# Decode attention over a 512 MB cache: loads of 8 MB for pairs of heads, `wo` loaded once at the end, MLP first

## The chip, the cores and the metric

The kernel runs on one NeuronCore of a Trainium2 chip. The metric is the device time of one execution in microseconds (us), the median of several runs. Before the change it is 1318.7 us (three runs, 1317.83 to 1319.73).

## What is computed

One decode step for two sequences. `x` (2 x 1 x 512) is layer-normalised to `xn`. Attention takes `q = xn @ wq` as 32 heads of 128, scores it against a cache of 8192 keys for each of the 64 (sequence, head) units, applies softmax, takes the weighted sum of 8192 values and multiplies by `wo`. A small MLP on the same `xn` makes a gate:

```
q = (xn @ wq) as [B=2, H=32, 1, Dh=128]
p = softmax(q . k_cache * Dh**-0.5)          # k_cache [2, 32, 8192, 128] float32
s = (p @ v_cache) as [2, 1, 4096] @ wo       # v_cache likewise, wo [4096, 512]
g = silu(gelu(layernorm(xn) @ w1 + b1) @ w2 + b2)
out = x + s * g
```

K and V are 268 MB each. With the weights the kernel reads 559.3 MB from device memory and writes 4 KB.

## The kernel before, in words

Everything is float32. The 64 units are taken in order, the two sequences of a head one after the other. A unit's keys are one tile of [128 partitions x 64 rows x 128], 4 MB: partition p holds rows 64p to 64p+63, so each partition's row in memory is 32 KB in one piece (`unit`, L50). `load_k` (L56) and `load_v` (L71) issue one transfer per unit from the SP queue. There are three K buffers and two V buffers of 32 KB per partition. `wo` comes in eight loads of 1 MB (`load_wo`, L60), one per four heads, in rows of 2 KB; the last head's 256 KB come by themselves at L325. The last unit's V comes in five pieces (L69).

Work of one unit:

- VectorE (DVE) multiplies the K tile in place by the query, which stands on every partition (L250), sums over the 128 elements (L254), and takes the row maximum (L256).
- TensorE (PE) transposes the 128 maxima (L260), DVE reduces them to one (L265), PE spreads it back (L270), and ScalarE (ACT) copies it and takes the exponential with a running sum (L272, L275). PE sums that over the partitions (L277) and DVE takes the reciprocal (L282).
- `weighted` (L285): sixteen matmuls with the probabilities as the stationary operand (128 x 4) and 512 columns of V moving, spread over four column groups of PE. Each appears as two records in the trace, so 32 records a unit.
- `project` (L296): ACT copies the result out of PSUM (L300), four small matmuls fold it to a column (L305), ACT scales it (L308). After the second sequence of a head four matmuls add its share of `wo` to `acc` (L314).

The order is written out by hand (L317 to L348), and each engine and each queue works in program order. In step i the SP queue gets the loads of K i+3 and V i+1; DVE multiplies unit i, PE and ACT do the softmax of unit i-1, DVE sums unit i, and PE weighs V of unit i-2. A load waits until its buffer is free: a K load until DVE has summed the unit that held the buffer, a V load until PE has weighed it. A load that waits holds back all later loads on SP.

Ahead of the loop come `x`, `wq` in two loads of 4 MB, K 0, `w1`, K 1, `w2`, K 2, the first `wo` and V 0; the layer norms; the projection of the queries (L163) and their spreading to all partitions, four heads at a time (L176). The MLP runs in pieces inside steps 0 to 2 (L339 to L343). After the loop the last unit is weighed, projected and added, then L355 and L356 multiply by the gate and add `x`, and four small stores (L359) end the kernel.

Of the kernel before, what the change touches and what calls it, by code (L numbers as in the profile page):

```python
# [19 lines left out]
def decode_kernel(ctx: ExitStack, tc: tile.TileContext, x, kc, vc, wq, wo, w1, b1, w2, b2, out):  # L20
# [18 lines left out]
    consts = ctx.enter_context(tc.tile_pool(name="consts", bufs=1))
    kpool = ctx.enter_context(tc.tile_pool(name="kpool", bufs=3))  # L40
    vpool = ctx.enter_context(tc.tile_pool(name="vpool", bufs=2))
    wpool = ctx.enter_context(tc.tile_pool(name="wpool", bufs=2))
    small = ctx.enter_context(tc.tile_pool(name="small", bufs=3))
    ps_c = ctx.enter_context(tc.tile_pool(name="ps_c", bufs=1, space=bass.MemoryType.PSUM))
    ps_w = ctx.enter_context(tc.tile_pool(name="ps_w", bufs=2, space=bass.MemoryType.PSUM))
    ps_s = ctx.enter_context(tc.tile_pool(name="ps_s", bufs=3, space=bass.MemoryType.PSUM))
# [3 lines left out]
    def unit(t, i):  # L50
        h, b = divmod(i, B)
        return t[b, h].rearrange("(p j) d -> p j d", p=P)

    K, V, WO = {}, {}, {}

    def load_k(i):  # L56
        K[i] = kpool.tile([P, KP, DH], F32, tag="k", name=f"k{i}")
        nc.sync.dma_start(K[i], unit(kc, i))

    def load_wo(g):  # L60
        t = wpool.tile([P, HG, D], F32, tag="w", name=f"wo{g}")
        src = wo[g * HG * DH:(g + 1) * HG * DH, :].rearrange("(h p) n -> p h n", p=P)
        n = HG if g < NG - 1 else HG - 1
        nc.sync.dma_start(t[:, :n, :], src[:, :n, :])
        WO[g] = t
        return t, src


    PIECES = [(0, 16), (16, 16), (32, 16), (48, 12), (60, 4)]  # L69

    def load_v(i):  # L71
        V[i] = vpool.tile([P, KP, DH], F32, tag="v", name=f"v{i}")
        if i < NU - 1:
            nc.sync.dma_start(V[i], unit(vc, i))  # L74
        else:
            for k0, n in PIECES:
                nc.sync.dma_start(V[i][:, k0:k0 + n, :], unit(vc, i)[:, k0:k0 + n, :])

    x_sb = consts.tile([B, D], F32, name="x_sb")
    nc.sync.dma_start(x_sb, x.rearrange("b s d -> (b s) d"))  # L80

    wq_v = wq.rearrange("(p c) n -> p c n", p=P)
    WQ = []
    for a in range(0, ND, 2):
        t = vpool.tile([P, 2, H * DH], F32, tag="v", name=f"wq{a}")
        nc.sync.dma_start(t, wq_v[:, a:a + 2, :])
        WQ.append(t)
    load_k(0)
    w1_sb = kpool.tile([P, ND, F], F32, tag="k", name="w1_sb")
    nc.sync.dma_start(w1_sb, w1.rearrange("(p c) f -> p c f", p=P))  # L90
    load_k(1)
    w2_sb = vpool.tile([P, NF + 1, D], F32, tag="v", name="w2_sb")
    nc.sync.dma_start(w2_sb[:, :NF, :], w2[:NF * P, :].rearrange("(p c) n -> p c n", p=P))
    nc.sync.dma_start(w2_sb[:FT, NF, :], w2[NF * P:, :])
    load_k(2)
    load_wo(0)
    load_v(0)
# [4 lines left out]
    b2_sb = consts.tile([1, D], F32, name="b2_sb")  # L102
    nc.vector.memset(x4, 0.0)
    nc.vector.memset(b1_sb, 0.0)
    for j in range(QT):
        nc.scalar.dma_start(x4[32 * j:32 * j + B, :], x[:, 0, j * P:(j + 1) * P])
# [7 lines left out]
    ones = consts.tile([P, P], F32, name="ones")  # L114
    nc.vector.memset(ones, 1.0)
    zeros = consts.tile([P, P], F32, name="zeros")
    nc.vector.memset(zeros, 0.0)
    srow = consts.tile([1, P], F32, name="srow")
# [4 lines left out]
    mask = consts.tile([P, JW], F32, name="mask")  # L123

    PO = [ps_c.tile([P, JW * DH], F32, name=f"po{n}") for n in range(2)]
    for t in PO:
        nc.vector.memset(t, 0.0)
    acc = ps_c.tile([P, P], F32, name="acc")


    def layernorm(src, name):
# [7 lines left out]
        dst = consts.tile([B, D], F32, name=name)  # L139
        nc.vector.tensor_scalar(dst, src, mv[:, 0:1], sd[:, 1:2], op0=ALU.subtract, op1=ALU.mult)  # L140
        return dst

    def transposed(src, name):
# [3 lines left out]
        for c in range(ND):  # L147
# [4 lines left out]
    xn = layernorm(x_sb, "xn")  # L152
    nc.vector.tensor_reduce(out=mask, in_=ident.rearrange("p (j r) -> p r j", r=32)[:, :JW, :],
                            axis=AX.X, op=ALU.add)
    y = layernorm(xn, "y")
# [3 lines left out]

    q_nat = consts.tile([P, NG // QT, 512], F32, name="q_nat")  # L160
    nc.gpsimd.memset(q_nat, 0.0)

    def project_q(n):  # L163
        p = ps_w.tile([P, 512], F32, tag="w", name=f"pq{n}")
        for c in range(ND):
            for j in range(QT):
                g = n * QT + j
                nc.tensor.matmul(p[32 * j:32 * j + B, :], xnT[:, c, :],  # L168
                                 WQ[c // 2][:, c % 2, g * 512:(g + 1) * 512],
                                 start=(c == 0), stop=(c == ND - 1))  # L170
        for j in range(QT):
            nc.scalar.copy(q_nat[32 * j:32 * j + B, n, :], p[32 * j:32 * j + B, :])  # L172

    Q = {}

    def queries(g):  # L176

        n, j = divmod(g, QT)
        q = small.tile([P, B, HG, DH], F32, tag="q", name=f"q{g}", bufs=2)
        for b in range(B):  # L180
            p = ps_w.tile([P, 512], F32, tag="w", name=f"pb{g}_{b}")
            r = 32 * j + b
            nc.tensor.matmul(p, ident[:, r:r + 1].to_broadcast([P, P]), q_nat[:, n, :], start=True, stop=True)  # L183
            nc.scalar.copy(q[:, b].rearrange("p h d -> p (h d)"), p)
        Q[g] = q

    project_q(0)
    queries(0)
    project_q(1)
    nc.tensor.matmul(acc, zeros, zeros, start=True, stop=False)  # L190


    gate = consts.tile([P, P], F32, name="gate")
    hT = consts.tile([P, NF + 1, B], F32, name="hT")
    G = {}

    def mlp_hidden():

        p = ps_s.tile([P, P], F32, tag="s", name="ph")
        nc.vector.memset(p[:, :(NF + 1) * B], 0.0)  # L200
        for f in range(NF + 1):
            for c in range(ND):
                w = w1_sb[:, c, f:NF * P:NF] if f < NF else w1_sb[:, c, NF * P:]
                nc.tensor.matmul(p[:w.shape[1], f * B:(f + 1) * B], w, yT[:, c, :],  # L204
                                 start=(c == 0), stop=(c == ND - 1))
        G["ph"] = p

    def mlp_gelu():
# [3 lines left out]
        p = G.pop("ph")[:, :(NF + 1) * B].rearrange("p (f b) -> p f b", b=B)  # L212
# [8 lines left out]

    def mlp_out():
        p = ps_s.tile([P, P], F32, tag="s", name="pgate")
        nc.tensor.matmul(p, zeros, zeros, start=True, stop=False)
        for f in range(NF + 1):
            m = P if f < NF else FT
            for j in range(QT):
                nc.tensor.matmul(p[32 * j:32 * j + B, :], hT[:m, f, :], w2_sb[:m, f, j * P:(j + 1) * P],
                                 start=False, stop=False)
        for j in range(QT):  # L230
            nc.tensor.matmul(p[32 * j:32 * j + B, :], ones[:1, :B], b2_sb[:, j * P:(j + 1) * P],
                             start=False, stop=True)
        G["pg"] = p

    def mlp_silu():
        z = small.tile([P, P], F32, tag="gz", name="gz", bufs=1)
        nc.scalar.copy(z, G.pop("pg"))
        th = small.tile([P, P], F32, tag="gt", name="gt", bufs=1)
# [4 lines left out]

    SC, PR, RS, RL, MX, OT = {}, {}, {}, {}, {}, {}

    def scores_mul(i):
        h, b = divmod(i, B)
        k = K[i]
        qb = Q[h // HG][:, b, h % HG, :].unsqueeze(1).to_broadcast([P, KP, DH])
        nc.vector.tensor_tensor(out=k, in0=k, in1=qb, op=ALU.mult)  # L250

    def scores_sum(i):
        SC[i] = small.tile([P, KP], F32, tag="sc", name=f"sc{i}")
        nc.vector.tensor_reduce(out=SC[i], in_=K.pop(i), axis=AX.X, op=ALU.add)  # L254
        MX[i] = small.tile([P, 1], F32, tag="mx", name=f"mx{i}")
        nc.vector.tensor_reduce(out=MX[i], in_=SC[i], axis=AX.X, op=ALU.max)  # L256

    def max_pe(i):
        p = ps_s.tile([P, P], F32, tag="s", name=f"pm{i}")
        nc.tensor.transpose(p[:1, :], MX[i], ident)  # L260
        MX[i] = p

    def max_dve(i):
        nm = small.tile([1, 1], F32, tag="nm", name=f"nm{i}")
        nc.vector.tensor_reduce(out=nm, in_=MX[i][:1, :], axis=AX.X, op=ALU.max, negate=True)  # L265
        MX[i] = nm

    def exps(i):
        p = ps_s.tile([P, P], F32, tag="s", name=f"pn{i}")
        nc.tensor.matmul(p[:, :1], srow, MX.pop(i), start=True, stop=True)  # L270
        bias = small.tile([P, 1], F32, tag="bias", name=f"bias{i}")
        nc.scalar.copy(bias, p[:, :1])  # L272
        PR[i] = small.tile([P, KP], F32, tag="pr", name=f"pr{i}")
        RS[i] = small.tile([P, 1], F32, tag="rs", name=f"rs{i}")
        nc.scalar.activation(PR[i], SC.pop(i), AF.Exp, bias=bias, scale=SCALE, accum_out=RS[i])  # L275
        pl = ps_s.tile([P, P], F32, tag="s", name=f"pl{i}")
        nc.tensor.matmul(pl[:, :1], ones, RS.pop(i), start=True, stop=True)  # L277
        RL[i] = pl
# [38 lines left out]
    for i in range(NU + 1):  # L317
# [8 lines left out]

        if i < NU:
            scores_mul(i)
# [58 lines left out]
```

## Time and profile before

| | |
|---|---|
| median of 3 runs | 1318.7 us |
| the profiled execution | 1319.86 us, of which the span from first to last instruction is 1318.1 us |
| busy share of the span | DVE 87%, PE 44% (weight loads 17%), ACT 8%, GpSimd 0% |
| mean share of the 16 DMA engines | 9 tenths or more in every slice of the span but the last (6 tenths) |
| read from device memory | 559.30 MB, mean 425 GB/s over the whole span |
| packets on SP's queue | 23948 |
| mean granted TensorE clock | 0.643 |

How to read it: the page cuts the span into 40 slices of 33 us. DMA share and GB/s per slice say whether the transfers ever stop. A row of part 5 is a group of instructions of one line: count, busy time, mean duration, then the idle time of the engine just before them and what ended most of it. The chain (part 4) is followed back from the last instruction to whatever released each step.

### The profile page before, as it was taken

How to read it: one execution, taken by the hardware profiler on the slowest of the kernel's cores; microseconds unless marked ns; L12 is line 12 of the kernel's file. 1: busy time of each engine (PE TensorE's matmuls, PEld its weight loads, DVE VectorE, ACT ScalarE, POOL GpSimd, SP SyncE). 2: the span in 40 equal slices, each digit the busy share in tenths (PEclk: the TensorE clock that was granted, in tenths of full speed). 3: DMA queues.
4: the chain of work that ended last, by engine and by line, in shares of the span. 5: the costliest groups of instructions: out<-in, count | busy, mean ns of one | idle time of the engine just before them, and what ended most of it. 6: DMA issues, size and time to landing. Idle time of an engine off the chain costs nothing.

```text
span 1318.1 us, 8108 instructions
## 1 busy us (share of the span) xinstructions
PE 586.5 (44%) x3434; PEld 226.1 (17%) x3434; DVE 1143.7 (87%) x348; ACT 110.7 (8%) x353; POOL 1.6 (0%) x7
## 2 busy tenths in 40 slices
PE   3554444335434344435435435435344345335336
PEld 0431111112111111111111112111111111111112
DVE  1789999888988988988988988988988889998983
ACT  1010010001000010000000001000000001000001
POOL 0000000000000000000000000000000000000000
PEclk9656676666567667576666567666566566666667
DMA  9999999999999999999999999999999999999996
GB/s 392 421 424 431 432 432 427 431 431 433 430 428 429 432 432 433 428 430 431 432 430 427 432 432 429 433 425 436 432 429 428 431 430 432 428 432 431 431 431 252
DMA packets 24266, 559.83 MB, mean 425 GB/s; under 512 B 2611, under 2 KB 2627, under 8 KB 7078
## 3 DMA queue, kind: packets, MB, share of 16 engines
q1 hardware_dynamic: 23948, 559.30, 99.1%
q8 instruction: 27, 0.44, 0.1%
q10 hardware_dynamic: 282, 0.01, 0.0%
q14 instruction: 9, 0.07, 0.0%
HBM read 559.30 MB, written 0.00 MB: 424 GB/s over the span
## 4 chain that ended last, share of the span: by engine, by line
DMA 64%; DVE 27%; PE 8%; ACT 1%; issue 0%; SPq 0%; DVEq 0%
DMA k<-in_A_k_cache_dram 55%; DVE k L250 15%; DVE sc L254 11%; DMA v<-in_A_v_cache_dram 8%; PE po L292 5%; PE ph L204 1%; DMA wq<-in_A_wq_dram 1%; PE pb L183 1%; PE pn L270 0%; PE pl L277 0%; PE pt L305 0%; ACT pr L275 0%; DVE nm L265 0%; SPq L74 0%; ACT o L300 0%
## 5 line engine op out<-in xcount | busy, mean ns | idle before, releaser
L250 DVE TENSOR_TENSOR k<-k,q 128x8192 f32<-128x8192 f32 x64 | 556.2, 8691 | 135.6 <-DMA k<-in_A_k_cache_dram 109.9
L254 DVE TENSOR_REDUCE sc<-k 128x64 f32<-128x8192 f32 x64 | 554.9, 8671 | 0.0
L292 PE MATMUL po<-v,pr 128*4 128x512 f32 x2046 | 353.6, 853 | 10.3 <-DMA v<-in_A_v_cache_dram 10.3
L270 PE MATMUL pn<-nm,srow 1*128 1x1 f32 x128 | 36.8, 354 | 571.7 <-DVE nm L265 571.7
L270 PEld LDWEIGHTS pn<-nm,srow 1*128 1x128 f32 x128 | 31.8, 307 | 585.3 <-DVE nm L265 423.7
L292 PEld LDWEIGHTS po<-v,pr 128*4 128x4 f32 x2046 | 58.0, 107 | 255.2 <-issue 243.5
L305 PE MATMUL pt<-mask,o 128*128 128x1 f32 x512 | 67.4, 253 | 45.7 <-ACT o L300 45.7
L305 PEld LDWEIGHTS pt<-mask,o 128*128 128x128 f32 x512 | 61.9, 191 | 108.1 <-ACT o L300 108.1
L300 ACT COPY o<-po 128x512 f32<-128x512 f32 x64 | 37.5, 586 | 395.4 <-PE po L292 395.4
L272 ACT COPY bias<-pn 128x1 f32<-128x1 f32 x64 | 10.2, 159 | 667.1 <-PE pn L270 667.1
L277 PE MATMUL pl<-rs,ones 128*128 128x1 f32 x128 | 37.5, 362 | 47.4 <-ACT pr L275 47.4
L277 PEld LDWEIGHTS pl<-rs,ones 128*128 128x128 f32 x128 | 32.0, 311 | 52.9 <-ACT pr L275 52.9
L183 PE MATMUL pb<-q_nat,ident 128*128 128x512 f32 x32 | 29.9, 1089 | 2.6 <-ACT q_nat L172 2.6
L265 DVE TENSOR_REDUCE nm<-pm 1x1 f32<-1x128 f32 x64 | 17.4, 272 | 13.4 <-PE pm L260 13.4
L204 PE MATMUL ph<-yT,w_sb 128*128 128x2 f32 (+1 forms) x88 | 19.5, 359 | 13.7 <-DVE ph L200 13.7
L308 ACT ACTIVATE oT<-pt,rl 128x1 f32<-128x1 f32 x64 | 16.7, 262 | 74.0 <-PE pt L305 71.7
L275 ACT ACTIVATE pr<-sc,bias 128x64 f32<-128x64 f32 x64 | 22.3, 348 | 2.1
L204 PEld LDWEIGHTS ph<-yT,w_sb 128*128 128x128 f32 (+1 forms) x88 | 19.4, 316 | 13.8 <-DVE ph L200 13.8
L314 PE MATMUL acc<-wo,oT 128*2 128x128 f32 x256 | 14.7, 307 | 11.2 <-ACT oT L308 11.2
L260 PE MATMUL pm<-ident,mx 128*1 128x128 f32 x64 | 18.6, 290 | 0.7 <-DVE mx L256 0.6
L168 PE MATMUL pq<-wq,xnT 128*2 128x512 f32 x64 | 11.7, 883 | 10.7 <-DMA wq<-in_A_wq_dram 10.7
L256 DVE TENSOR_REDUCE mx<-sc 128x1 f32<-128x64 f32 x64 | 14.1, 220 | 2.2
(65 smaller groups left out, 83.9 us busy)
## 6 DMA issues: line engine op xcount, KB each, us to landing
k<-in_A_k_cache_dram SPq DMA_DIRECT2D x64, 4096.0 KB, 40.8
v<-in_A_v_cache_dram SPq DMA_DIRECT2D x63, 4096.0 KB, 32.3
wq<-in_A_wq_dram SPq DMA_DIRECT2D x2, 4096.0 KB
wo<-in_A_wo_dram SPq DMA_DIRECT2D x7, 1024.0 KB, 43.4
v<-in_A_v_cache_dram SPq DMA_DIRECT2D x3, 1024.0 KB, 9.0
w_sb<-in_B_w_dram SPq DMA_DIRECT2D x1, 2752.0 KB
w_sb<-in_B_w_dram SPq DMA_DIRECT2D x1, 2560.0 KB
wo<-in_A_wo_dram SPq DMA_DIRECT2D x1, 768.0 KB, 42.4
```

Source lines behind the costliest of these rows:

```text
L183: nc.tensor.matmul(p, ident[:, r:r + 1].to_broadcast([P, P]), q_nat[:, n, :], start=True, stop=True)
L204: nc.tensor.matmul(p[:w.shape[1], f * B:(f + 1) * B], w, yT[:, c, :], start=(c == 0), stop=(c == ND - 1))
L250: nc.vector.tensor_tensor(out=k, in0=k, in1=qb, op=ALU.mult)
L254: nc.vector.tensor_reduce(out=SC[i], in_=K.pop(i), axis=AX.X, op=ALU.add)
L260: nc.tensor.transpose(p[:1, :], MX[i], ident)
L265: nc.vector.tensor_reduce(out=nm, in_=MX[i][:1, :], axis=AX.X, op=ALU.max, negate=True)
L270: nc.tensor.matmul(p[:, :1], srow, MX.pop(i), start=True, stop=True)
L275: nc.scalar.activation(PR[i], SC.pop(i), AF.Exp, bias=bias, scale=SCALE, accum_out=RS[i])
L277: nc.tensor.matmul(pl[:, :1], ones, RS.pop(i), start=True, stop=True)
L292: nc.tensor.matmul(po[32 * j:32 * j + JW, :], PR[i][:, t * JW:(t + 1) * JW], v[:, t * JW:(t + 1) * JW, :].rearrange("p j d -> p (j d)"), s ...
L300: nc.scalar.copy(o4, PO[i % 2])
L305: nc.tensor.matmul(pt[:, :1], lhsT, rhs, start=(n == 0), stop=(n == len(terms) - 1))
```

## The change

The unit becomes a pair of neighbouring heads of one sequence (n = 0 to 31, the first sequence's sixteen pairs first). Its K and its V are one load of 8 MB each: 128 partitions with 128 rows of 128, one head on partitions 0 to 63 and the other on 64 to 127, 64 KB in one piece per partition. Two buffers of 64 KB per partition hold K (and at first `wq`, at the end V 30 and `wo`), one holds V (and at first all that the MLP and the projection need, in `boot`).

- DVE's two large operations are done in halves of 64 rows, so each keeps the shape it had (128 x 8192); per pair there are two multiplies and two sums. The first pair's K comes in two halves.
- The softmax steps run once per pair: one transpose, one maximum with two results, two small matmuls, one copy, two exponentials on 64 partitions each, written into a tile `PZ` that is zero elsewhere, so that one matmul with 8 stationary columns weighs both heads. `weighted` is now 32 matmuls per pair.
- The heads' results are not multiplied by `wo` one by one. `columns`, `spread` and `place` put each pair's result into a PSUM tile `OA` that is laid out for one multiplication at the end; the denominators are collected there too. `wo` is one tile of 64 KB rows, in five pieces, the last load of the kernel; 128 matmuls on it follow the last pair.
- The MLP runs whole before the projection, with `w1` and `w2` loaded before `wq`. `load_k(1)` and `load_v(0)` stand behind the projection in SP's queue.
- In the loop, step n issues on SP `load_v(n)` once pair n-1 is weighed, and `load_k(n+2)` at its end; the last steps have an order of their own (`LATE` is 30).

The core of the diff:

```diff
+    U = 2
+    HP = P // U
+    KP = S // HP
+    HH = H // U
+    N = B * HH
...
+    kpool = ctx.enter_context(tc.tile_pool(name="kpool", bufs=2))
+    vpool = ctx.enter_context(tc.tile_pool(name="vpool", bufs=1))
...
+    def load_k(n, cuts=(0, KP)):
+        K[n] = kpool.tile([P, KP, DH], F32, tag="k", name=f"k{n}")
+        load(K[n], kf[n], cuts)
+
+    def load_v(n, cuts=(0, KP), pool=vpool, tag="v"):
+        V[n] = pool.tile([P, KP, DH], F32, tag=tag, name=f"v{n}")
+        load(V[n], vf[n], cuts)
+
+
+    PIECES = (0, 32, 64, 96, 112, 128)
+    WO_PIECES = (0, 8, 16, 24, 29, 32)
...
+    wq_sb = kpool.tile([P, ND, H * DH], F32, tag="k", name="wq_sb")
+    boot = vpool.tile([P, KP * DH], F32, tag="v", name="boot")
...
     nc.sync.dma_start(x_sb, x.rearrange("b s d -> (b s) d"))
 
     nc.sync.dma_start(w1_sb, w1.rearrange("(p c) f -> p c f", p=P))
     nc.sync.dma_start(w2_sb[:, :NF, :], w2[:NF * P, :].rearrange("(p c) n -> p c n", p=P))
     nc.sync.dma_start(w2_sb[:FT, NF, :], w2[NF * P:, :])
+    nc.sync.dma_start(wq_sb, wq.rearrange("(p c) n -> p c n", p=P))
+    load_k(0, (0, KP // 2, KP))
...
+    mlp()
...
+    for n in range(NG // QT):
+        project_q(n)
+    gather_q()
+    queries(0)
+    load_k(1)
+    load_v(0)
...
+    def exps(n):
+        p = ps_s.tile([P, P], F32, tag="s", name=f"pn{n}")
+        nm = MX.pop(n)
+        for s in range(U):
+            nc.tensor.matmul(p[HP * s:HP * (s + 1), :1], srow, nm[:, s:s + 1], start=True, stop=True)
+        bias = small.tile([P, 1], F32, tag="bias", name=f"bias{n}")
         nc.scalar.copy(bias, p[:, :1])
+        rs = small.tile([P, 1], F32, tag="rs", name=f"rs{n}")
+        sc = SC.pop(n).rearrange("p (t j) -> p t j", j=JW)
+        for s in range(U):
+            r = slice(HP * s, HP * (s + 1))
+            nc.scalar.activation(PZ[n % 3][r, :, s, :], sc[r], AF.Exp, bias=bias[r], scale=SCALE,
+                                 accum_out=rs[r])
+
+        nc.scalar.activation(ZR[:, ZP:P], half, AF.Copy, scale=rs)
...
+        nc.tensor.matmul(OA[:, b, OC:], ZR[:, a:a + P], ones[:, :1], start=False, stop=False)
+
+    def weighted(n):
+        po, v, pz = PO[n % 2], V.pop(n), PZ[n % 3]
+        for t in range(NT):
             j = t % QT
+            nc.tensor.matmul(po[R * j:R * j + U * JW, :], pz[:, t].rearrange("p s j -> p (s j)"),
                              v[:, t * JW:(t + 1) * JW, :].rearrange("p j d -> p (j d)"),
+                             start=(t < QT), stop=(t + QT >= NT))
...
+    M = KP // 2
+    LATE = N - 2
+    for n in range(N):
+        scores_mul(n, 0, M)
+        if n:
+            max_dve(n - 1)
+            if n < LATE:
+                exps(n - 1)
+        scores_mul(n, M, KP)
+        if n + 1 < N:
+            queries(n + 1)
+
+
+        m = None
+        if 1 <= n < LATE - 1 or n >= LATE:
+            m = n - 1 if n < LATE else n - 2
+            weighted(m)
+            columns(m)
+            if m + 1 < LATE - 1:
+                load_v(m + 1)
+            elif n == LATE:
+                load_v(N - 3)
+            elif n == N - 1:
+                load_v(N - 1, PIECES)
+        if n >= LATE:
+            exps(n - 1)
+
+        scores_sum(n, 0, M)
+        if n == N - 1:
+            spread(m)
+            place(m)
+            weighted(n - 1)
+            columns(n - 1)
+            m = n - 1
+        scores_sum(n, M, KP)
+        max_rows(n)
+        max_pe(n)
+        if m is not None:
+            spread(m)
+            place(m)
+
+
+        if n + 2 < N:
+            load_k(n + 2)
+        elif n == LATE:
+            load_v(n, pool=kpool, tag="k")
+        if n == LATE - 2:
+            load_v(n)
+
+    wo_sb = kpool.tile([P, OC, D], F32, tag="k", name="wo_sb")
+    load(wo_sb, wo.rearrange("(p c) n -> p c n", p=P), WO_PIECES)
+
+    n = N - 1
+    max_dve(n)
+    exps(n)
+    weighted(n)
+    columns(n)
+    spread(n)
+    place(n)
...
+    for c in range(OC):
+        for j in range(QT):
+            nc.tensor.matmul(acc[R * j:R * j + B, :], on[:, :, c], wo_sb[:, c, j * P:(j + 1) * P],
+                             start=(c == 0), stop=(c == OC - 1))
```

More of the change, by code (lines that the diff above doesn't have):

```diff
@@ L71, in load_v @@
[L71 to L79, printed above, removed]
-    nc.sync.dma_start(x_sb, x.rearrange("b s d -> (b s) d"))
[L82 to L87, printed above, removed]
@@ L88, in decode_kernel, with load @@
-    load_k(0)
-    w1_sb = kpool.tile([P, ND, F], F32, tag="k", name="w1_sb")
+    K, V = {}, {}
+    kf = kc.rearrange("b h s d -> (b h s d)").rearrange("(n p j d) -> n p j d", p=P, j=KP, d=DH)
+    vf = vc.rearrange("b h s d -> (b h s d)").rearrange("(n p j d) -> n p j d", p=P, j=KP, d=DH)
+    def load(dst, src, cuts):
+        for a, e in zip(cuts, cuts[1:]):
+            nc.sync.dma_start(dst[:, a:e], src[:, a:e])
+    def load_k(n, cuts=(0, KP)):
+        K[n] = kpool.tile([P, KP, DH], F32, tag="k", name=f"k{n}")
+        load(K[n], kf[n], cuts)
@@ new lines, in load_v, with take @@
+    def load_v(n, cuts=(0, KP), pool=vpool, tag="v"):
[5 more added lines that the diff above has]
+    boot = vpool.tile([P, KP * DH], F32, tag="v", name="boot")
+    used = [0]
+    def take(p, n):
+        a = used[0]
+        used[0] += n
+        assert used[0] <= KP * DH
+        return boot[:p, a:a + n]
@@ L90, in decode_kernel @@
+    w1_sb = take(P, ND * F).rearrange("p (c f) -> p c f", f=F)
+    w2_sb = take(P, (NF + 1) * D).rearrange("p (c n) -> p c n", n=D)
+    x_sb = take(B, D)
+    xn = take(B, D)
+    y = take(B, D)
+    b2_sb = take(1, D)
+    q_nat = take(P, NG // QT * 512).rearrange("p (n c) -> p n c", c=512)
+    sel = take(P, P)
+    z = take(P, P)
+    th = take(P, P)
+    nc.sync.dma_start(x_sb, x.rearrange("b s d -> (b s) d"))
     nc.sync.dma_start(w1_sb, w1.rearrange("(p c) f -> p c f", p=P))
-    load_k(1)
@@ L121, in decode_kernel, with layernorm @@
     nc.vector.memset(eps_t, EPS)
-    mask = consts.tile([P, JW], F32, name="mask")
+    mod = consts.tile([P, R], F32, name="mod")
+    blk = consts.tile([P, QT], F32, name="blk")
+    half = consts.tile([P, U * PH], F32, name="half")
+    nc.vector.memset(half, 0.0)
+    for s in range(U):
+        nc.vector.memset(half[HP * s:HP * (s + 1), PH * s:PH * (s + 1)], 1.0)
+    Z = consts.tile([P, 2 * P - U * PH], F32, name="Z")
+    ZR = consts.tile([P, 2 * P - U * PH], F32, name="ZR")
+    nc.gpsimd.memset(Z, 0.0)
+    nc.gpsimd.memset(ZR, 0.0)
+    PZ = [consts.tile([P, NT, U, JW], F32, name=f"pz{n}") for n in range(3)]
+    for t in PZ:
+        nc.gpsimd.memset(t, 0.0)
     PO = [ps_c.tile([P, JW * DH], F32, name=f"po{n}") for n in range(2)]
-    for t in PO:
+    acc = ps_c.tile([P, P], F32, name="acc")
+    OA = ps_c.tile([P, B, OC + 1], F32, name="OA")
+    for t in PO + [acc]:
         nc.vector.memset(t, 0.0)
-    acc = ps_c.tile([P, P], F32, name="acc")
-    def layernorm(src, name):
+    zeros = PZ[2].rearrange("p t s j -> p (t s j)")
+    nc.tensor.matmul(OA.rearrange("p b c -> p (b c)"), zeros[:, :P], zeros[:, :B * (OC + 1)],
+                     start=True, stop=False)
+    def layernorm(dst, src, name):
         st = small.tile([B, nc.vector.BN_STATS_DIM], F32, tag="st", name=f"st_{name}")
@@ L150, in transposed, with mlp @@
         return t
[L152 to L155, printed above, removed]
+    layernorm(xn, x_sb, "xn")
+    by_row = ident.rearrange("p (j r) -> p r j", r=R)
+    nc.vector.tensor_reduce(out=mod, in_=by_row, axis=AX.X, op=ALU.add)
+    nc.vector.tensor_reduce(out=blk, in_=ident.rearrange("p (j r) -> p j r", r=R), axis=AX.X, op=ALU.add)
+    layernorm(y, xn, "y")
     xnT = transposed(xn, "xn")
     yT = transposed(y, "y")
[L160 to L190, printed above, removed]
     gate = consts.tile([P, P], F32, name="gate")
     hT = consts.tile([P, NF + 1, B], F32, name="hT")
[L195 to L200, printed above, removed]
+    def mlp():
+        ph = ps_s.tile([P, P], F32, tag="s", name="ph")
+        nc.vector.memset(ph[:, :(NF + 1) * B], 0.0)
         for f in range(NF + 1):
@@ L280, in denominator @@
-    def denominator(i):
-        rl = small.tile([P, 1], F32, tag="rl", name=f"rl{i}")
-        nc.vector.reciprocal(rl, RL[i][:, :1])
-        RL[i] = rl
-    def weighted(i, t0, t1, nt=NT):
-        po, v = PO[i % 2], V[i]
-        for t in range(t0, t1):
+    mlp()
+    nc.gpsimd.memset(q_nat, 0.0)
+    nc.vector.memset(sel, 0.0)
+    nc.vector.tensor_copy(
+        sel[:, HP:].rearrange("p (b j r) -> p b j r", b=B, r=HG)[:, :, :QT, 0], by_row[:, :B, :])
+    q_all = consts.tile([B * H, DH], F32, name="q_all")
@@ new lines, in project_q, with gather_q @@
+    def project_q(n):
+        p = ps_s.tile([P, 512], F32, tag="s", name=f"pq{n}")
+        for c in range(ND):
+            for j in range(QT):
+                g = n * QT + j
+                nc.tensor.matmul(p[R * j:R * j + B, :], xnT[:, c, :], wq_sb[:, c, g * 512:(g + 1) * 512],
+                                 start=(c == 0), stop=(c == ND - 1))
+        for j in range(QT):
+            nc.scalar.copy(q_nat[R * j:R * j + B, n, :], p[R * j:R * j + B, :])
+    def gather_q():
+        p = ps_s.tile([P, P], F32, tag="s", name="pqa")
+        for n in range(NG // QT):
+            for hh in range(HG):
+                a = HP - (n * QT * HG + hh)
+                nc.tensor.matmul(p[:B * H, :], sel[:, a:a + B * H], q_nat[:, n, hh * DH:(hh + 1) * DH],
+                                 start=(n + hh == 0), stop=(n == NG // QT - 1 and hh == HG - 1))
+        nc.scalar.copy(q_all, p[:B * H, :])
@@ new lines, in decode_kernel, with queries @@
+    Q = {}
+    def queries(n):
+        p = ps_s.tile([P, P], F32, tag="s", name=f"pb{n}")
+        for s in range(U):
+            w = ident[:B * H, U * n + s:U * n + s + 1].to_broadcast([B * H, HP])
+            nc.tensor.matmul(p[HP * s:HP * (s + 1), :], w, q_all, start=True, stop=True)
+        Q[n] = small.tile([P, DH], F32, tag="q", name=f"q{n}")
+        nc.scalar.copy(Q[n], p)
+    for n in range(NG // QT):
+        project_q(n)
[3 more added lines that the diff above has]
+    load_v(0)
@@ new lines, in decode_kernel, with scores_mul, scores_sum, max_rows @@
+    SC, MX, PT = {}, {}, {}
+    def scores_mul(n, a, e):
+        k = K[n][:, a:e, :]
+        qb = Q[n].unsqueeze(1).to_broadcast([P, e - a, DH])
+        nc.vector.tensor_tensor(out=k, in0=k, in1=qb, op=ALU.mult)
+    def scores_sum(n, a, e):
+        if a == 0:
+            SC[n] = small.tile([P, KP], F32, tag="sc", name=f"sc{n}")
+        nc.vector.tensor_reduce(out=SC[n][:, a:e], in_=K[n][:, a:e, :], axis=AX.X, op=ALU.add)
+    def max_rows(n):
+        MX[n] = small.tile([P, 1], F32, tag="mx", name=f"mx{n}")
+        nc.vector.tensor_reduce(out=MX[n], in_=SC[n], axis=AX.X, op=ALU.max)
@@ L317, in decode_kernel @@
-    for i in range(NU + 1):
-        if i + 3 < NU:
-            load_k(i + 3)
-        if i + 1 < NU:
-            if (i + 1) % UG == 0:
-                tail = load_wo((i + 1) // UG)
-            load_v(i + 1)
-        if i == NU - 2:
-            nc.sync.dma_start(tail[0][:, HG - 1, :], tail[1][:, HG - 1, :])
-        if i < NU:
-            scores_mul(i)
-        if i >= 1:
-            max_pe(i - 1)
-            max_dve(i - 1)
-            exps(i - 1)
-        if i < NU:
-            scores_sum(i)
-        if i >= 1:
-            denominator(i - 1)
-        if i == 0:
-            mlp_hidden()
-        if i == 1:
-            mlp_gelu()
-            mlp_out()
-        if i == 2:
-            mlp_silu()
-        if i % UG == UG - 2 and i // UG + 1 < NG:
-            queries(i // UG + 1)
-        if i >= 2:
-            weighted(i - 2, 0, NT)
-            project(i - 2)
@@ L350, in decode_kernel, with columns @@
-    i = NU - 1
-    weighted(i, 0, NT - 1, NT - 1)
-    project(i, direct=(KP - JW, KP))
+                             start=(t < QT), stop=(t + QT >= NT))
+    def columns(n):
+        o4 = small.tile([P, JW * DH], F32, tag="o4", name=f"o4_{n}", bufs=1)
+        nc.scalar.copy(o4, PO[n % 2])
+        PT[n] = ps_s.tile([P, P], F32, tag="s", name=f"pt{n}")
+        for i in range(JW):
+            nc.tensor.matmul(PT[n][:, :U], o4[:, i * DH:(i + 1) * DH], mod[:, i:U * JW:JW],
+                             start=(i == 0), stop=(i == JW - 1))
@@ new lines, in spread, with place @@
+    def spread(n):
+        shape = [P, U, PH]
+        nc.vector.tensor_tensor(out=Z[:, ZP:P].rearrange("p (s r) -> p s r", s=U),
+                                in0=blk.unsqueeze(1).to_broadcast(shape),
+                                in1=PT.pop(n)[:, :U].unsqueeze(2).to_broadcast(shape), op=ALU.mult)
+    def place(n):
+        b, hp = divmod(n, HH)
+        a = ZP - U * PH * hp
+        nc.tensor.matmul(OA[:, b, :OC], Z[:, a:a + P], mod, start=False, stop=(n == N - 1))
+    M = KP // 2
+    LATE = N - 2
@@ new lines, in decode_kernel @@
+    wo_sb = kpool.tile([P, OC, D], F32, tag="k", name="wo_sb")
[7 more added lines that the diff above has]
+    place(n)
+    rl = consts.tile([P, B], F32, name="rl")
+    nc.vector.reciprocal(rl, OA[:, :, OC])
+    on = consts.tile([P, B, OC], F32, name="on")
+    nc.vector.tensor_tensor(out=on, in0=OA[:, :, :OC], in1=rl.unsqueeze(2).to_broadcast([P, B, OC]), op=ALU.mult)
+    for c in range(OC):
+        for j in range(QT):
+            nc.tensor.matmul(acc[R * j:R * j + B, :], on[:, :, c], wo_sb[:, c, j * P:(j + 1) * P],
+                             start=(c == 0), stop=(c == OC - 1))
```

130 lines of the change are left out of this document (30 added, 100 removed).

## The prediction

> **What bounds the kernel now.** I read the slices of the page first, then the chain, then the timeline of DVE's multiplies, then the last 30 us in windows.
>
> ```profile
> DVE  1789999888988988988988988988988889998983
> DMA  9999999999999999999999999999999999999996
> GB/s 392 421 424 431 432 432 427 431 431 433 430 428 429 432 432 433 428 430 431 432 430 427 432 432 429 433 425 436 432 429 428 431 430 432 428 432 431 431 431 252
> DMA k<-in_A_k_cache_dram 55%; DVE k L250 15%; DVE sc L254 11%; DMA v<-in_A_v_cache_dram 8%; PE po L292 5%; PE ph L204 1%; DMA wq<-in_A_wq_dram 1%; PE pb L183 1%; PE pn L270 0%; PE pl L277 0%; PE pt L305 0%; ACT pr L275 0%; DVE nm L265 0%; SPq L74 0%; ACT o L300 0%
> ```
>
> The DMA engines are busy in every slice but the last, at about 431 GB/s. DVE is nearly as full (87%), but waits for K: the chain is mostly K loads, and DVE's two steps stand in it only because they free buffers early enough. So the time is bytes over rate, plus a start and an end in which no transfer runs. Three things can change it: bytes, rate, ends.
>
> The rate, from the starts of L250 (start us, duration; in brackets the idle time before it and what ended it):
>
> ```profile
> 385.06 8.69 DVE L250 TENSOR_TENSOR k<-k,q 128x8192 f32<-128x8192 f32 x1 [1.69 <-DMA k<-in_A_k_cache_dram]
> 407.11 8.69 DVE L250 TENSOR_TENSOR k<-k,q 128x8192 f32<-128x8192 f32 x1 [4.24 <-DMA k<-in_A_k_cache_dram]
> ...
> 1239.09 8.69 DVE L250 TENSOR_TENSOR k<-k,q 128x8192 f32<-128x8192 f32 x1 [1.71 <-DMA k<-in_A_k_cache_dram]
> 1258.51 8.69 DVE L250 TENSOR_TENSOR k<-k,q 128x8192 f32<-128x8192 f32 x1 [1.61 <-DMA k<-in_A_k_cache_dram]
> ```
>
> One unit's K and V (8.389 MB) take 19.43 us in most steps (here 1258.51 - 1239.09 = 19.42). Where a 1 MB load of `wo` lies between, the step is longer (407.11 - 385.06 = 22.05; six such steps 22.05 to 22.40, mean 22.16). So 1.049 MB in rows of 2 KB cost 2.73 us, where K's rate would give 2.43.
>
> **A price per row.** Call it a, on each of the 16 DMA engines, beside a pure rate r. K and V of a unit: 524 KB per engine in 16 rows, 524.3/r + 16a = 19.43. One `wo` load: 65.5 KB in 32 rows, 65.5/r + 32a = 2.73. These give a = 0.010 us and r = 27.2 KB/us per engine, 435 GB/s over 16; 8.389 MB without rows would take 19.27 us. A load of 8.389 MB in rows of 64 KB (8 per engine) then takes 19.27 + 0.08 = 19.35 us. No row in the trace is longer than 32 KB, so this is bounded: 19.43 if a long row is cut in two, 19.27 if the overhead vanished. I take 19.35, which the fit gives.
>
> **The end now:**
>
> ```profile
> 1285.00:1290.00 5.00, 2.12 (x12) 1.25 (x16) 5.00 (x3) 0.60 (x3) 0.00 (x0) 0.50 0.97 419
> 1290.00:1295.00 5.00, 5.00 (x28) 0.74 (x20) 5.00 (x1) 0.00 (x0) 0.00 (x0) 0.55 0.69 295
> 1295.00:1300.00 5.00, 2.84 (x25) 1.96 (x21) 1.19 (x4) 1.45 (x5) 0.00 (x0) 0.79 0.83 310
> 1300.00:1305.00 5.00, 5.00 (x26) 1.04 (x29) 0.17 (x1) 0.00 (x0) 0.00 (x0) 0.52 1.00 422
> 1305.00:1310.00 5.00, 4.28 (x44) 1.70 (x39) 0.00 (x0) 0.85 (x2) 0.00 (x0) 1.00 0.54 215
> ```
>
> The last column is GB/s. Transfers end near 1305 + 5 x 215/431 = 1307.5, and 10.6 us follow: the last unit is weighed, projected and added. Between 1290 and 1300 a hole of about 3.0 us stands (5 - 5 x 295/431, and the same for 310), because the last V load waits for unit 61 to be weighed.
>
> **The change, part by part.**
>
> *Bytes.* Follow the loads of V through the loop. At n = 28, m is 27, m + 1 = 28 is below LATE - 1 = 29, so `load_v(28)` is issued; at the end of the same step `n == LATE - 2` holds, and `load_v(28)` is issued again. The first copy is never read: `weighted(28)` in step 30 reads the second. V 28 comes twice: 8.389 MB, **+19.35 us**, unless transfers stood still there anyway, and they don't (below). The repeat must wait on SP for the first copy's landing; behind it waits only K 31, whose turn comes two loads later.
>
> *Rows of K and V.* 64 x (19.43 - 19.35) = **-5.1 us** (bounds 0 and -10.2).
>
> *wo.* Before 8 x 2.73 = 21.8; after 19.27 + 40 rows x 0.010 = 19.7: **-2.2 us** (the wider pieces cost little). The pieces of the last V and the halves of K 0 add 0.2. Bytes and rows together: 19.35 - 5.1 - 2.2 + 0.2 = **+12.2 us**.
>
> *The end.* `wo` is last and needs nothing but small matmuls. Counting from the start of the first V 28, with 19.35 per load: V 31's last piece lands near 136; it is weighed by about 140 (a unit's 32 records took 3.6 to 6.4 us), folded and placed (L300 0.59, L305 1.05 and a few of 0.3) by 143; the last piece of `wo` lands near 156, 13 us later. Then three of 32 column groups are left, 24 records at the 0.40 us per 8 that L314 took, 1.2 us. From L314 to the end of the span took 1318.1 - 1314.4 = 3.7 us before, of which 0.4 is L314 itself. With 1 us of landing, the estimate is 1.0 + 1.2 + 3.3 = 5.5 to 6, taken as 5.8, against 10.6: **-4.8 us** (bounds -3 and -6). The hole of 3.0 us goes too if V 31 is issued in time: pair 29 is weighed by about 107, its buffer's turn is at 116: **-3.0 us**.
>
> *Steady state.* A pair needs two loads, 38.7 us. DVE: four times 8.7 and three small steps, 35.6. The weighing of a pair: 64 records, 7.2 to 12.8 us from the same rows, and it starts when V lands; so `load_v` of the next pair is issued 5 us or more before the K load ahead of it has run out (19.35 - 12.8 - 1). The next K load is issued when DVE ends a pair, some 20 us ahead of need. Softmax steps, halved in number, lie beside transfers before and after: nothing gained or lost.
>
> *The start.* `w1` (2.8 MB) lands near 10 us, the hidden layer takes 19.5 us (the L204 row), GELU 1.5 and a table load 1.3, the output layer 4.9 (L228, L231): 38 us. `wq` has landed at 36 by then. The projection takes 7 to 13.7 us (64 records; sixteen took 3.59 at first, thirty-two 4.53 later), the copies and the gathering some 6. DVE starts pair 0 at 52 to 59 and ends it at 87 to 94. K 2's turn comes at 94.4, after K 0, K 1 and V 0. So the start just fits; I put no hole there, with 0 to 7 us as its bounds (K 2 late by 2, V 1 by 5, where PE is slow throughout).
>
> **Sum against the profiled execution:** 12.2 - 4.8 - 3.0 = +4.4 us: span 1318.1 to 1322.5, time 1319.9 to 1324.3. The median was 1.2 below the profiled run: **1323 us**. What a measurement of this kernel can tell from no change is about 0.2%, 2.6 us, so "slower" begins at 1321.3. With the bounds above this case alone runs from 1317 to 1330.
>
> **Rivals.**
>
> *The repeated load costs nothing* (not slower). Nothing reads the first copy; if the program that runs doesn't contain that transfer, everything else stays: 1323 - 19.35 = 1304. For it: no result depends on it. Against it: every load in the code before appears in the transfer table (64 + 63 + 5 pieces), and nothing there shows that an unread one would be left out. It decides if 33 V transfers of 8 MB become 32; short of that, the other gains must exceed 19.35 + 2.6, where I find 15.
>
> *One V buffer makes holes* (slower). Before, several loads were queued (40.8 us from issue to landing, four loads of 9.7); now the V load is issued 5 to 9 us before its turn. For it: the start is tight, and the hole at 1290 to 1300 shows what a late V load costs. Against it: 12.8 us is the slowest the rows allow. If the start slips by its full 7 us: 1330; if a hole of 1 us came in every third step: 1334.
>
> *A row pitch of 64 KB is slower.* The second half of `wq`, read at that pitch, came in 9.89 us (13.32 to 23.21) where half a K and V pair takes 9.72, 1.8% more; on all K and V that is +22 us, 1345. Against it: from 25 to 60 us K and `w1` came at 425 GB/s too, as `wq` did from 5 to 25, so this is the start and not the pitch. The Trainium skill, "DMA: Bandwidth & Descriptors", section "Latency and other measured facts", speaks for this rival: rows spaced by large powers of two slow a copy, 207 GB/s at a pitch of 512 KiB where a padded one gives 214; by that 3.3% an estimate would be +41 us, 1364. Its list does not reach down to 64 KB, and no run here shows a larger pitch.
>
> **Chances.** The forecast's case 0.76 (slower 0.53, within 0.2% 0.21, faster 0.02); the repeat costs nothing 0.10; holes 0.11; pitch 0.03. So slower 0.67, same 0.21, faster 0.12. Range 1317 to 1334: the forecast's own range and the holes; the repeat that costs nothing and the pitch are left out.
>
> **What would show it.** Two transfers of V 28 around K 30, 567.7 MB read instead of 559.3, about 11,400 packets on SP's queue; L250 of successive pairs 38.7 us apart; no slice below 425 GB/s but the first and last; the last piece of `wo` some 5.8 us before the end. It is wrong if the bytes stay at 559.3 MB, if the step is 38.86 (rows cut in two) or above 39 (holes, pitch), or if `load_v` waits on PE with no transfer running.

## The result, and the profile after

| | before | after |
|---|---|---|
| median | 1318.67 us (4 runs, 1317.83 to 1319.73) | 1326.98 us (4 runs, 1326.06 to 1327.77) |
| profiled execution, span | 1319.86, 1318.1 us | 1327.17, 1325.4 us |
| read from device memory | 559.30 MB | 567.69 MB |
| packets on SP's queue | 23948 | 11356 |

The changed kernel is slower: ratio 1.0062, 95% interval 1.0045 to 1.008. The forecast was 1323.

The page of the changed kernel, rate per slice, SP's queue and the chain:

```profile
GB/s 391 442 433 426 437 436 430 431 436 431 434 433 436 432 429 438 431 434 431 434 434 435 428 433 440 429 430 436 435 427 436 438 427 432 438 437 425 434 420 312
q1 hardware_dynamic: 11356, 567.68, 99.2%
DMA v<-in_A_v_cache_dram 69%; PE po L323 21%; DMA wo_sb<-in_A_wo_dram 2%; DMA wq_sb<-in_A_wq_dram 2%; DVE k L275 2%; DVE sc L280 1%; DMA boot<-in_B_w_dram 1%; PE pq L237 1%; ACT boot L240 0%; PE pqa L247 0%; PE pb L258 0%; ACT pz L308 0%; PE acc L415 0%; PE OA L314 0%; PE pn L301 0%
```

The transfers run through, a little faster than before (most slices 430 to 438 where 428 to 433 stood; one near the end, 420, lies below the 425 that the prediction named), and yet the time is longer: 8.39 MB more are read. The chain now names V loads and PE's weighing (L323, 21%), since each V load waits for the one buffer to be weighed. That share is no lost time: while PE weighs, a K load is in flight. The timeline of SP's loads shows by how much:

```profile
1075.92 0.33 SPq L60 DMA_DIRECT2D v<-in_A_v_cache_dram  x1
1082.77 0.33 SPq L60 DMA_DIRECT2D k<-in_A_k_cache_dram  x1
...
1153.87 0.33 SPq L60 DMA_DIRECT2D v<-in_A_v_cache_dram  x1
1160.16 0.33 SPq L60 DMA_DIRECT2D k<-in_A_k_cache_dram  x1
1183.45 0.33 SPq L60 DMA_DIRECT2D v<-in_A_v_cache_dram  x1
1198.87 0.33 SPq L60 DMA_DIRECT2D k<-in_A_k_cache_dram  x1
```

The V load at 1075.92 is issued 10.8 us before the K load ahead of it lands (DVE starts on that K at 1086.76, in the next lines). The last four lines are V 28, K 30, V 28 again and K 31: the second copy is issued at 1183.45, as the first has landed.

And DVE's multiplies, two pairs running (the first half of each):

```profile
1048.07 8.69 DVE L275 TENSOR_TENSOR k<-k,q 128x8192 f32<-128x8192 f32 x1 [3.64 <-DMA k<-in_A_k_cache_dram]
...
1086.76 8.69 DVE L275 TENSOR_TENSOR k<-k,q 128x8192 f32<-128x8192 f32 x1 [3.63 <-DMA k<-in_A_k_cache_dram]
```

A step is 38.69 us; two units of the kernel before took 38.86. DVE waits 3.6 us in it, for K.

### The profile page after: what moved, and what is told of

Read it like the earlier page. It is cut to its first block, busy times and chain, and to the rows that moved or that the text cites. A ratio compares the mean times of both kernels' runs of the same rounds, so it can differ in the third digit from the quotient of the medians.

```text
span 1325.4 us, 7362 instructions
## 1 busy us (share of the span) xinstructions
PE 444.6 (34%) x3250; PEld 173.4 (13%) x3250; DVE 1129.0 (85%) x261; ACT 82.4 (6%) x274; POOL 2.8 (0%) x12
## 3 DMA queue, kind: packets, MB, share of 16 engines
q1 hardware_dynamic: 11356, 567.68, 99.2%
HBM read 567.69 MB, written 0.00 MB: 428 GB/s over the span
## 4 chain that ended last, share of the span: by engine, by line
DMA 74%; PE 22%; DVE 3%; ACT 0%; issue 0%; SPq 0%
DMA v<-in_A_v_cache_dram 69%; PE po L323 21%; DMA wo_sb<-in_A_wo_dram 2%; DMA wq_sb<-in_A_wq_dram 2%; DVE k L275 2%; DVE sc L280 1%; DMA boot<-in_B_w_dram 1%; PE pq L237 1%; ACT boot L240 0%; PE pqa L247 0%; PE pb L258 0%; ACT pz L308 0%; PE acc L415 0%; PE OA L314 0%; PE pn L301 0%
## 5 line engine op out<-in xcount | busy, mean ns | idle before, releaser
L275 DVE TENSOR_TENSOR k<-k,q 128x8192 f32<-128x8192 f32 x64 | 555.5, 8681 | 116.8 <-DMA k<-in_A_k_cache_dram 103.3
L323 PE MATMUL po<-v,pz 128*8 128x512 f32 x2048 | 294.7, 740 | 236.2 <-DMA v<-in_A_v_cache_dram 236.2
L323 PEld LDWEIGHTS po<-v,pz 128*8 128x8 f32 x2048 | 57.3, 104 | 455.8 <-DMA v<-in_A_v_cache_dram 247.7
L330 ACT COPY o<-po 128x512 f32<-128x512 f32 x32 | 18.8, 586 | 528.9 <-PE po L323 528.9
L333 PE MATMUL pt<-mod,o 128*128 128x2 f32 x256 | 33.7, 254 | 22.9 <-ACT o L330 22.9
L333 PEld LDWEIGHTS pt<-mod,o 128*128 128x128 f32 x256 | 31.0, 191 | 52.6 <-ACT o L330 52.6
L314 PE MATMUL OA<-ones,ZR 128*128 128x1 f32 x64 | 18.6, 360 | 51.8 <-ACT ZR L311 51.8
L308 ACT ACTIVATE pz<-sc,bias 64x128 f32<-64x128 f32 x64 | 25.5, 399 | 1.4
L258 PE MATMUL pb<-q_all,ident 64*64 64x128 f32 x128 | 21.3, 433 | 0.3 <-ACT q_all L249 0.3
L192 PE MATMUL ph<-yT,boot 128*128 128x2 f32 (+1 forms) x88 | 19.5, 359 | 1.6 <-DMA boot<-in_B_w_dram 1.6
L192 PEld LDWEIGHTS ph<-yT,boot 128*128 128x128 f32 (+1 forms) x88 | 19.4, 317 | 1.6 <-issue 1.6
```

The source lines that it names most:

```text
L192: nc.tensor.matmul(ph[:w.shape[1], f * B:(f + 1) * B], w, yT[:, c, :], start=(c == 0), stop=(c == ND - 1))
L258: nc.tensor.matmul(p[HP * s:HP * (s + 1), :], w, q_all, start=True, stop=True)
L308: nc.scalar.activation(PZ[n % 3][r, :, s, :], sc[r], AF.Exp, bias=bias[r], scale=SCALE, accum_out=rs[r])
L314: nc.tensor.matmul(OA[:, b, OC:], ZR[:, a:a + P], ones[:, :1], start=False, stop=False)
L323: nc.tensor.matmul(po[R * j:R * j + U * JW, :], pz[:, t].rearrange("p s j -> p (s j)"), v[:, t * JW:(t + 1) * JW, :].rearrange("p j d -> p ...
L330: nc.scalar.copy(o4, PO[n % 2])
```

## The experiments

The theory: the time is the sum of what the 16 DMA engines carry, at 19.27 us per 8.389 MB and about 0.010 us per row and engine, plus the ends; the repeat of V 28 costs its whole transfer. Rival A puts the loss on waits (the single V buffer, the order of the last steps), rival B says that the repeat filled time in which nothing would have run. A second question is why the forecast was 4 us short.

**once** and **once_early**: V 28 comes once, behind or ahead of K 30.

```diff
-            if m + 1 < LATE - 1:
+            if m + 1 < LATE - 2:
```

> Changed kernel, but the first copy of V 28 (the one that nothing reads) isn't loaded; V 28 comes once, behind K 30. Theory (the repeat costs exactly its transfer): 1327.0 - 19.35 = 1307.6 us, 559.3 MB read, steps of 38.70 us. Rival A (the time is lost in waits at the single V buffer and in the order of the last steps): most of it stays, 1318 or more. Rival B (the repeat filled time in which the transfers would have stood still): about 1327.

```diff
-        if n == LATE - 2:
-            load_v(n)
```

> Changed kernel, but the second copy of V 28 isn't loaded; V 28 comes once, ahead of K 30. Theory: which copy goes doesn't matter, since K 31 and V 29 are still issued before their turn: 1307.6 us, within 1 of the run without the first copy. Rival A (the order of the last steps is what costs): the two runs differ by several us.

Measured: 1308.4 us (ratio to the kernel before 0.9919, interval 0.9904 to 0.9933) and 1307.3 (0.9912, 0.9897 to 0.9926); both read 559.30 MB. The repeat costs 18.6 or 19.6 us, one transfer of 19.35. Both rivals fall. The place of V 28 matters by 1.1 us at most, and the runs of the two kernels overlap. Without the repeat the kernel beats the one before by 10 to 12 us.

**half**: the first copy is half as long.

```diff
-                load_v(m + 1)
+                load_v(m + 1, (0, KP // 2) if m + 1 == LATE - 2 else (0, KP))
```

> Changed kernel, but the first copy of V 28 is only half of each partition's rows (64 of 128, 4 MB). Theory: half the cost, 1327.0 - 9.7 = 1317.3 us. Rival A: as the changed kernel, 1326 to 1327, since the order of the loads and all waits stay. Rival B: 1327.

Measured: 1317.1 us. The loads stand in the same order as in the changed kernel, and 9.9 us are gone for 4.19 MB. The cost follows the bytes.

**repeat10**: a repeat in the middle of the loop, for the price of a true hole.

```diff
-            if m + 1 < LATE - 1:
+            if m + 1 < LATE - 2:
...
-        if n == LATE - 2:
+        if n in (10, LATE - 2):
```

> As the run without the first copy of V 28, but V 10 is loaded twice in the middle of the loop, the second time behind K 12. Here V 11 stands behind the weighing of pair 10, and K 13 behind V 11 on SP, so nothing is in flight when the second copy has landed. Theory: 19.35 for the transfer and a hole of 9.2 (weighing) plus about 2 (issue to first data), 11 us, in sum 1307.6 + 30.5 = 1338 us; one step of L275 is 69 us instead of 38.7. If a late V load costs nothing, because K 12 and K 13 are ahead: 1327.

Measured: 1339.9 us (two runs), 31.5 above `once`. Its windows (last columns: clock, DMA share, GB/s):

```profile
510.00:520.00 10.00, 0.00 (x0) 0.00 (x0) 0.00 (x0) 0.00 (x0) 0.00 (x0) 0.50 0.97 419
520.00:530.00 10.00, 6.89 (x44) 1.41 (x48) 0.00 (x0) 0.00 (x0) 0.00 (x0) 0.61 0.02 7
530.00:540.00 10.00, 4.19 (x35) 1.77 (x27) 5.71 (x2) 0.58 (x1) 0.00 (x0) 0.73 0.80 315
```

From 523, where the second copy has landed, to 530 nothing is transferred while PE weighs pair 10. L275 starts 69.25 us after the pair before instead of 38.70:

```profile
465.12 8.69 DVE L275 TENSOR_TENSOR k<-k,q 128x8192 f32<-128x8192 f32 x1 [4.27 <-DMA k<-in_A_k_cache_dram]
...
534.37 8.69 DVE L275 TENSOR_TENSOR k<-k,q 128x8192 f32<-128x8192 f32 x1
```

So this is what a V load that comes too late costs, 11 to 12 us; the changed kernel has no such window. Its repeat stands where K 31 comes before the next V.

**rows32** and **rows16**: the same loads cut into transfers with shorter rows.

```diff
-    def load_k(n, cuts=(0, KP)):
+    def load_k(n, cuts=(0, KP // 2, KP)):
...
-    def load_v(n, cuts=(0, KP), pool=vpool, tag="v"):
+    def load_v(n, cuts=(0, KP // 2, KP), pool=vpool, tag="v"):
```

(`rows16` has the cuts 0, KP // 4, KP // 2, 3 * KP // 4, KP; both are made from `once`.)

> As the run without the first copy of V 28, but each load of K and V comes as two transfers of 4 MB with rows of 32 KB (the last V keeps its pieces). Theory (a price of 0.010 us per row on each DMA engine): 8 rows more per engine and load, 63 x 0.08 = +5.0 us, 1312.6; steps of 38.86. Rival (only bytes count): 1307.6 and steps of 38.70. Rival (larger loads gain by a fixed cost per load of 2 us): +126 us.

> The same with four transfers of 2 MB and rows of 16 KB. Theory: 24 rows more per engine and load, 63 x 0.24 = +15 us, 1322.7; steps of 39.18. Rival (only bytes count): 1307.6. If the price is per transfer and not per row the ratio to the run with two transfers is the same 3 to 1, so this run tells the size, not the kind.

Measured: 1311.9 and 1321.6 us, 3.5 and 13.2 above `once`. The steps are the sharper measure: 38.85 and 39.16 us at the median, against 38.70. First `rows32`, then `rows16`, each with two pairs running:

```profile
739.57 8.69 DVE L275 TENSOR_TENSOR k<-k,q 128x8192 f32<-128x8192 f32 x1 [0.77 <-DMA k<-in_A_k_cache_dram]
...
778.42 8.69 DVE L275 TENSOR_TENSOR k<-k,q 128x8192 f32<-128x8192 f32 x1 [0.77 <-DMA k<-in_A_k_cache_dram]
```

```profile
734.80 8.69 DVE L275 TENSOR_TENSOR k<-k,q 128x8192 f32<-128x8192 f32 x1 [3.13 <-DMA k<-in_A_k_cache_dram]
...
773.97 8.69 DVE L275 TENSOR_TENSOR k<-k,q 128x8192 f32<-128x8192 f32 x1 [3.14 <-DMA k<-in_A_k_cache_dram]
```

16 rows more per engine and pair cost 0.15 us, 48 more 0.46: 0.0095 us a row in both. But the number of loads grew with the number of rows, by 2 and by 6 a pair, so 0.08 us a load would fit as well. These two runs can't tell a price per row from one per load; the next one can.

**b_wo8**: the kernel before, `wo` in rows of 8 KB, in as many loads.

```diff
-        src = wo[g * HG * DH:(g + 1) * HG * DH, :].rearrange("(h p) n -> p h n", p=P)
+        src = wo[g * HG * DH:(g + 1) * HG * DH, :].rearrange("(p h) n -> p h n", p=P)
```

> The kernel before, with wo loaded in rows of 8 KB instead of 2 KB (each partition takes four neighbouring rows, so the heads are multiplied by the wrong rows of wo; all amounts stay). Theory (0.010 us per row): 24 rows fewer per engine and load, 8 x 0.24 = -1.9 us, 1316.8; the steps with a wo load 21.92 instead of 22.16. Rival (only bytes count): 1318.7.

Measured: 1317.0 us, ratio 0.9988 (0.998 to 0.9997), 0.4 to 2.6 us less than before. The steps with a `wo` load:

```profile
386.20 8.69 DVE L250 TENSOR_TENSOR k<-k,q 128x8192 f32<-128x8192 f32 x1 [1.64 <-DMA k<-in_A_k_cache_dram]
408.12 8.69 DVE L250 TENSOR_TENSOR k<-k,q 128x8192 f32<-128x8192 f32 x1 [4.10 <-DMA k<-in_A_k_cache_dram]
```

They take 21.86 to 21.92 us where 22.05 to 22.40 were needed: with the same number of loads, 24 rows fewer per engine are faster by about 0.2 us a load, 0.009 us a row (the longest steps before also carry the drift that is told below). That is close to the price of a row found above, and it leaves next to nothing for a fixed price per load.

**b_v63**: the kernel before with its hole closed.

```diff
-        V[i] = vpool.tile([P, KP, DH], F32, tag="v", name=f"v{i}")
+        pool, tag = (kpool, "k") if i == NU - 1 else (vpool, "v")
+        V[i] = pool.tile([P, KP, DH], F32, tag=tag, name=f"v{i}")
```

> The kernel before, with one edit: the last V (unit 63) goes into a K buffer that is free by then, so its load no longer waits for unit 61 to be weighed, and the hole between 1290 and 1300 us should close. Theory (the hole was in the mean of the 16 DMA engines; the slowest, which sets every landing, never stopped): the time stays, 1318.7 within 0.5. Rival, as the prediction had it (the hole is lost time): -3.0 us, 1315.7.

Measured: 1318.0 us, ratio 0.9993 (0.9985 to 1.0002), between 2.0 less and 0.3 more than before; the 3.0 of the prediction lie outside. Its last windows:

```profile
1290.00:1295.00 5.00, 5.00 (x32) 0.84 (x24) 5.00 (x1) 0.00 (x0) 0.00 (x0) 0.62 0.97 415
1295.00:1300.00 5.00, 2.84 (x24) 1.78 (x20) 1.63 (x4) 1.45 (x5) 0.00 (x0) 0.72 0.97 403
1300.00:1305.00 5.00, 5.00 (x30) 1.26 (x34) 0.17 (x1) 0.00 (x0) 0.00 (x0) 0.60 0.80 326
1305.00:1310.00 5.00, 4.28 (x40) 1.61 (x35) 0.00 (x0) 0.85 (x2) 0.00 (x0) 1.00 0.21 79
```

The hole is closed (415 and 403 GB/s where 295 and 310 stood) and has moved to the end (326 and 79 where 422 and 215 stood). The last transfer lands at 1308.6, before at 1308.4. The next section says why.

**wo_whole** and **v31_whole**: the last loads without pieces, made from `once_early`.

```diff
-    WO_PIECES = (0, 8, 16, 24, 29, 32)
+    WO_PIECES = (0, 32)
```

> As the run without the second copy of V 28 (1307.3 us), but wo comes in one transfer instead of five. Theory (the end is short because all but the last piece of the product on wo is done while wo still lands): the 128 matmuls on wo, 256 records, all follow the landing; at 1.93 to 2.6 us per 64 records that is 7.7 to 10.4 us instead of 0.84, less 0.3 for 32 rows fewer per engine: +6.6 to +9.3, 1314 to 1316.6. Rival (the end is set by folding the last pair): no change, 1307.

```diff
-    PIECES = (0, 32, 64, 96, 112, 128)
+    PIECES = (0, 128)
```

> As the run without the second copy of V 28 (1307.3 us), but the last V comes in one transfer instead of five. Theory (some 13 us of slack between the last pair and the last piece of wo): the weighing starts when all of V 31 has landed, 9.2 us later than the first pieces allowed, still ahead of wo's fourth piece; 32 rows fewer per engine save 0.3: 1307.0. Rival (the end is set by folding the last pair): +5 us, 1312.

Measured: 1314.9 and 1307.4 us. With `wo` whole, all 256 records follow its landing:

```profile
1300.51 9.20 PE L413 MATMUL acc<-wo_sb,on 128*2 128x128 f32 x256 [11.93 <-DMA wo_sb<-in_A_wo_dram]
```

That is 7.5 us lost. With V 31 whole, the last pair is ready for `wo` at 1293.3 instead of 1289.7, and nothing is lost: PE catches up while `wo` still lands. The end of the kernel is set by the landing of `wo`, and what follows it is short only because of the pieces.

## Why the prediction was right, and where it was not

The kernel is slower and its time lies in the range, by the mechanism that was given: one more load of V costs more than the longer rows and the shorter end give back. The size was short. The medians moved by 8.3 us where 4.4 were forecast. Of the 3.9 us between them 3.0 are the hole (below), and 1.0 comes from the profiled executions from which the sum was made: the one before lay 1.2 us above its median, the one after 0.2.

**Bytes: right.** The two copies of V 28 stand in the timeline, and a whole, a half and no first copy give 1327.0, 1317.1 and 1307.3 to 1308.4 us.

**Rows of K and V: right.** Forecast 19.35 us per load; the step of 38.70 is twice that. The packets on SP's queue fell to 11356, as forecast for rows of 64 KB in one piece. The Trainium skill, "DMA: Bandwidth & Descriptors", section "Why a DMA increments its semaphore by 16 and not by 1", says that one descriptor moves one contiguous run; the trace agrees: the packets are 10,080 rows, 8,192 of them of 64 KB, and sixteen completion counts for each of some 80 loads. The rival of the row pitch falls: at 64 KB the loads are no slower, but 0.4% faster.

***wo*: right, slightly large.** Forecast -2.2 us for 216 rows fewer per engine; the run with rows of 8 KB, which takes away some 190 of them, was 1.6 us faster (0.4 to 2.6). The 2.73 us per load in the prediction is a mean of steps some of which carry the drift.

**The end: right, slightly small.** Forecast -4.8, from 10.6 to 5.8. From the last landing to the end of the span it was 1318.1 - 1308.4 = 9.7 us and is now 1325.4 - 1321.0 = 4.4, so -5.3. Both ends were shorter than thought. Before, the last landing came 0.9 us later than the 1307.5 that was read from the rate. After, the 1 us set aside for landing is not there: PE starts on the last piece 0.05 us after it has landed at 1321.03.

```profile
1321.08 0.84 PE L415 MATMUL acc<-wo_sb,on 128*2 128x128 f32 x24 [1.09 <-DMA wo_sb<-in_A_wo_dram]
```

**The start and the steady state: right.** K 2 was issued at 86.6, at the early edge of the 87 to 94 that were given, and before its turn, which came near 94.4. DVE needs 35.0 us a pair and not 35.6 (its first steps are 34.97 apart), and weighing a pair takes 9.2 us, inside the 7.2 to 12.8.

**The hole: wrong.** The step that failed is "the hole of 3.0 us goes too". Closing the hole alone, in `b_v63`, changed the time by -0.9 us, in an interval from -2.0 to +0.3 that holds zero and leaves out -3.0. The 295 and 310 GB/s were a mean over 16 DMA engines, and the engines are not equally far. Each load's semaphore rises sixteen times in the trace. The Trainium skill, "DMA: Bandwidth & Descriptors", section "Why a DMA increments its semaphore by 16 and not by 1", says that each of the engines counts once, when its own part has landed. First and last of these counts, in us:

| load | first | last | apart |
|---|---|---|---|
| before, K 0 | 32.56 | 33.80 | 1.2 |
| before, V 61 | 1282.21 | 1287.82 | 5.6 |
| before, V 63, fourth piece | 1306.59 | 1307.11 | 0.5 |
| b_v63, V 63, fourth piece | 1301.03 | 1307.31 | 6.3 |
| after, last piece of `wo` | 1314.22 | 1321.03 | 6.8 |

The fastest engine is 5.6 us ahead when V 61 lands. At 1291.9 it has finished all that is queued and stands still until V 63 is issued at 1295.4, which is the hole. The slowest is at V 62 until 1297.5, 2.1 us after that issue, and loses 0.2 us: its next count, of the first piece of V 63, comes 2.7 us later, where the pieces behind it take 2.5. Only when the slowest has delivered its part does a load count as landed. Closing the hole lets the fast engines finish 5.6 us earlier (in `b_v63` the first count of the kernel's last load, of `wo`, comes at 1302.4 instead of 1307.9), and the last count comes at nearly the same moment. Without this term the forecast's sum is 12.2 - 4.8 = +7.4 us, 1325.5 for the span and 1326 for the median; measured were +7.3 and 1327.0. That the span agrees to 0.1 us is partly luck: the last landing moved by 12.6 us and the end by -5.3, and the two misses cancel.

**Why the slowest engine falls behind.** In the changed kernel the first counts of successive loads stay 19.35 us apart nearly throughout, while the spread of a load's counts grows over the run from about 2 to 5 us. It grows in jumps: two pairs of steps together lose 1.6 us each (39.02 and 39.95 near 450, 39.06 and 39.90 near 915, instead of 38.70). The first of these pairs:

```profile
387.02 8.69 DVE L275 TENSOR_TENSOR k<-k,q 128x8192 f32<-128x8192 f32 x1 [3.64 <-DMA k<-in_A_k_cache_dram]
...
426.04 8.69 DVE L275 TENSOR_TENSOR k<-k,q 128x8192 f32<-128x8192 f32 x1 [3.96 <-DMA k<-in_A_k_cache_dram]
...
465.98 8.69 DVE L275 TENSOR_TENSOR k<-k,q 128x8192 f32<-128x8192 f32 x1 [4.89 <-DMA k<-in_A_k_cache_dram]
```

The jumps go with a second queue, which the page lists as

```profile
q8 instruction: 25, 0.41, 0.1%
```

These are 25 packets of 16 KB; by the queue's name they carry the program's instructions. Seventeen of them start between 200 and 1240 us, and behind each one, one of a load's sixteen counts comes 1.4 to 1.6 us later against the others than it did before, and this lasts. Mostly that engine is still ahead of the last one, and no step changes. Behind the packets at 411.8 and 454.2 us, and behind those at 877.9 and 920.2, the engine becomes the last, and the four long steps follow. Another packet, at 1318.6, stands ahead of the landing of the last piece of `wo`, whose counts lie 6.8 us apart after 5.6 for the piece before it. The trace doesn't name the engine of a packet, and no run has fewer of these packets, so this cause is read from the order in time and not shown by an experiment.

## What to carry to other kernels

Before rewriting loads for a better rate, count them: 64 loads of K and V became 65, and one unread copy cost more (19.35 us) than longer rows, a better last load and a shorter end together gave (some 11). A dip in the mean DMA rate is lost time only if the slowest engine stands still; look at whether the last landing moves, or at the first and last completion count, before booking it as a gain. In a kernel at the DMA limit the last load should be the one that least work follows, cut in pieces so that this work is mostly done when it lands.

## What the runs showed that was not expected

The sixteen DMA engines drift apart, from 1.2 us at the first loads of the kernel before to 5 to 7 us after 1300 us, by jumps of some 1.5 us of one engine that follow packets on the queue `q8 instruction`. In these runs with full queues they don't come together again; a pause of the fast ones brings them together (0.5 us after the hole). A step's time is that of the slowest engine: 39.95 us where two first counts take 38.70. The price of a row, 0.0095 us on each engine, is the same from rows of 16 KB to 64 KB, and fits the rows of 2 KB within 10%.
